# Renamed second-layer blocks, an order repaired piece by piece, and block sums on GpSimd in a channel attention and FFN kernel

## The chip, the cores and the metric

The kernel runs on one core of a Trainium2 chip. The metric is device time in microseconds, as the median of several executions; a separate profiled execution gives the trace that is read here. The engines are TensorE (PE; PEld are its weight loads), the Vector engine (DVE), the Scalar engine (ACT), GpSimd (POOL) and SyncE (SP), which issues all DMAs.

## The reference

Four batches of N = 6080 tokens with C = 256 channels go through channel attention and then a two-layer network with 2048 hidden columns, all in float32:

```python
qn = q / (np.linalg.norm(q, axis=1, keepdims=True) + 1e-06)
kn = k / (np.linalg.norm(k, axis=1, keepdims=True) + 1e-06)
s = kn.transpose(0, 2, 1) @ qn / tau
a = np.exp(s - s.max(-1, keepdims=True))
a /= a.sum(-1, keepdims=True) + 1e-09
x = (v @ a).reshape(B * N, C)
h = x @ w_in
g = 0.5 * h * (1.0 + erf(h / sqrt(2)))
return g @ w_out
```

## The kernel before

The attention matrix of a batch is folded into the first layer's weights, so that the rest is h = v (a w_in), a gelu, and g w_out. Every float32 operand is split into a high and a low half of the matmul's format, and each product is three matmuls (high by low weight, high by high, low by high weight).

Both layers use a seven-product scheme on blocks of 2 x 2 (Strassen-Winograd): each operand's blocks A11 to A22 or B11 to B22 are joined to sums S1 to S4 and T1 to T4, seven products P1 to P7 are formed in place of eight, and their sums are the result. A batch's tokens are cut into chunks of 512 or 480 tokens (twelve a batch, `CHUNKS`; the last two, from `WIDE` = 10 on, are "wide" and use plain products in the second layer), and the hidden columns into four groups g of 512 (`NWG`). One step of the main loop is one (batch b, chunk c, group g).

In a step, `chunk_ops` issues the seven first-layer products (`do`, 42 matmuls of 256 columns), whose results gather in the PSUM tiles pa or pb ("one" and "two"), px ("x") and pz ("z"). The four blocks of the gelu's input are complete in this order: x after product 3, p5 after product 4, z after product 5, "one" after product 6. Scalar applies gelu to each twice, once to the high half `his` (`gelu_hi`) and once in full to `gs` (`gelu_whole`); Vector subtracts for the low half `los` (`lo`). For the second layer there are two forms:

- *crossed*: Vector forms T1 to T4 from the four blocks in `gs` (`t_add`), Scalar casts them to high halves (`t_hi`), Vector makes the low halves (`t_lo`); the seven products take 42 matmuls of 256 columns in `chunk_out` (L1122 to L1124), with seven of the eight stored weight forms, in four loads to the ring of four `wo` tiles.
- *plain*: no T blocks; B12 gets its own high and low half, and eight products take 24 matmuls of 512 columns (L1106 to L1108), with four weight forms in two loads.

Which is used is told by `plain_out`: plain in the wide chunks, in chunk 2 of batch 0, and in the last group (g = 3) of those chunks for which `MIXED` holds, before for all. The matmuls of a step's second layer stand between the first-layer products of the next step. At a chunk's end `join_ops` sums the products' accumulators (banks po0 to po3) in the tile `osb`; where the last group is plain, two banks are read by Scalar copies and two by Vector additions, otherwise three by copies.

Beside this, v's blocks of the next chunk are summed (`v_sums`: one instruction of 512 elements and two of 256, to the tile vs, L834 to L838) and split into halves (`v_hi`, `v_lo`), the scores and norms of the next batch are formed in bursts (`burst`, `split_hi`, `split_lo`), and at a batch's end the new first-layer weights are summed (`w_adds`, four instructions of 256 elements a group, L771 to L774). All of these sums are on the Vector engine; GpSimd only writes constants at the start.

The order on each engine is made while the kernel is built. All instructions from the first weights on are recorded with their tiles (`Order.arrange`), and `schedule` runs a list planner over them: for each instruction a due time `late`, from the order of the matmuls, which is fixed; `run` plays all engines through with the planner's costs; for every stall of TensorE, `late` of the chain that caused it is set earlier, and the whole is run again, 24 times (`ROUNDS`), keeping the best order.

Of the kernel before, what the change touches and what calls it, by code (L numbers as in the profile page):

```python
# [16 lines left out]
P = 128  # L17
# [38 lines left out]
BLOCK = {(1, 0): "B22", (0, 1): "B11", (1, 1): "B21", (0, 0): "B12"}  # L56

PE, ACT, DVE, SP = (mybir.EngineType.PE, mybir.EngineType.Activation, mybir.EngineType.DVE, mybir.EngineType.SP)

# [21 lines left out]
class Order:  # L81
# [32 lines left out]
    def cost(self, ins, reads, writes):  # L114
        n = max([x[3] for x in reads + writes] + [1])
        psum = any(x[0][0] in ("pa", "pb", "px", "pz", "po0", "po1", "po2", "po3") for x in reads)
        if ins.engine == PE:
            k = reads[0][3] if reads else 1
            if ins.ins[0].dtype == F32:
                return (max(1.69 * k, 112.0),) * 2  # L120
            return max(.4167 * k + 2.8, 111.7), .4167 * k + 170
        if ins.engine == DVE:
            t = n / .96 + 66
            if len([x for x in reads if x[3] > 1]) < 2 and not psum:
                t = n / 1.92 + 66
            return t, t + 90
        if ins.engine == ACT:
            t = .855 * n + (48 if psum else 80)
            return t + 90 * (len(ins.outs) > 1), t + 105
        return 60, n * 512 / BANDWIDTH  # L130


    def arrange(self, body, start):


        todo = [i for i in body[start:] if i.engine in (PE, ACT, DVE, SP)]
        state = {}
# [47 lines left out]
    def schedule(self, todo, preds, costs):  # L185


        n = len(todo)
        self.engine = [(PE, ACT, DVE, SP).index(i.engine) for i in todo]
        self.preds, self.costs = preds, costs  # L190
# [27 lines left out]
        late = self.latest(t + 1e4)  # L218
        best = None
        for _ in range(ROUNDS):  # L220
            end, order, starts, last = self.run(late)
            if best is None or end < best[0]:
                best = end, order
            for p, q in zip(line, line[1:]):
                stall = starts[q] - starts[p] - costs[p][0]
                if stall > 30:
                    a, hops = last[q], 0
                    while a >= 0 and self.engine[a] and hops < 12:
                        late[a] -= min(1500, stall)
                        a, hops = last[a], hops + 1  # L230
        return best[1]

# [16 lines left out]

    def run(self, late):  # L250
        import heapq
        n = len(self.preds)
        left = [len(p) for p in self.preds]
        ready, starts, last = [0.0] * n, [0.0] * n, [-1] * n
        known = [[] for _ in range(4)]
        for a in range(n):
            if not left[a]:
                known[self.engine[a]].append(a)
        table = "Gelu"
        free, order, slip, dma, events = [0.0] * 4, [], 0.0, 0.0, [0.0]  # L260
        while len(order) < n:
# [3 lines left out]
            for e in range(4):  # L265
                if free[e] > now or not known[e]:
# [37 lines left out]
        return max(starts), order, starts, last  # L304


ROUNDS = 24

WAIT = {PE: 58, ACT: 34, DVE: 40, SP: 0}

# [3 lines left out]
def MIXED(b, c):  # L314
    return True

# [21 lines left out]
def channel_attention_gelu_ffn(ctx, tc, qk, kqt, vt, tau, w_in, w_out, out):  # L338
# [490 lines left out]
    def v_sums(b, c, pieces=(0, 1)):  # L829
        x, h = v_half(b, c)  # L830
        tt = nc.vector.tensor_tensor
        if 0 in pieces:
            t = vts[b, c] = pv.tile([P, 4, H], F32, name="vs")
            tt(out=t[:, 0:2, :h], in0=x[:, :, 1], in1=x[:, 0], op=ALU.subtract)  # L834
        if 1 in pieces:
            t = vts[b, c]
            tt(out=t[:, 2, :h], in0=x[:, 1, 1], in1=t[:, 0, :h], op=ALU.subtract)
            tt(out=t[:, 3, :h], in0=x[:, 1, 0], in1=t[:, 2, :h], op=ALU.subtract)  # L838
# [85 lines left out]
    def slots(n, c, g):  # L924
        at = p_slot(n, c, g)
        return {"B12": at, "B11": at + 1, "B22": 4 if c >= WIDE and g % 2 == 0 else 5, "B21": 6}

# [91 lines left out]

    SOURCE = {"B22": "x", "B11": "p5", "B21": "z", "B12": "one"}  # L1020

# [33 lines left out]
    def chunk_out(b, c, g, n):  # L1055
# [7 lines left out]
        if c >= WIDE:  # L1063
# [66 lines left out]
    def join_ops(b, c):  # L1130
# [24 lines left out]
        def join(i):  # L1155
# [4 lines left out]
            elif i == "u23":  # L1160
                tt(out=o[:, 2:4], in0=o[:, 6:4:-1], in1=p6.unsqueeze(1).broadcast_to([P, 2, h]), op=ALU.add)
            elif i == "c1":
                tt(out=o[:, 0:2], in0=banks(0), in1=o[:, 2:5:2], op=ALU.add)
            elif i == "c1s":
                tt(out=o[:, 0:2], in0=o[:, 0:2], in1=o[:, 2:5:2], op=ALU.add)
            elif i == "c22":
                tt(out=o[:, 2], in0=o[:, 2], in1=p7, op=ALU.add)
            elif i == "c2":
                tt(out=o[:, 2:4], in0=banks(1), in1=o[:, 2:4], op=ALU.add)
            elif i == "c21":  # L1170
                tt(out=o[:, 3], in0=banks(1)[:, 1], in1=o[:, 3], op=ALU.add)
            else:
# [42 lines left out]
    def narrow_unit():  # L1215
# [8 lines left out]
        else:  # L1224
# [4 lines left out]
            v = f32(wo).rearrange("p h i (c n) -> p i c h n", c=NCT)  # L1229
            for at, i, c in ((1, 0, 0), (2, 1, 0), (6, 0, 1), (7, 1, 1)):  # L1230
                keep(keep_out[form][:, at, :, q], v[:, i, c])
# [215 lines left out]
    for n, (b, c, g) in enumerate(steps):  # L1447
# [55 lines left out]
    for n, (b, c, g) in enumerate(steps):  # L1503
# [47 lines left out]
        at(e[4] + 1.85, lo, "B11")
        spread(n, "dve3", e[4] + 2.45)
        at(e[5] + .4, gelu_hi, "B21")
        at(e[5] + .9, gelu_whole, "B21")
        at(e[5] + 1.5, lo, "B21")
        at(e[6] + .1, gelu_whole, "B12")
# [73 lines left out]
```

## Time and profile before

| | before |
|---|---|
| median of 3 runs | 2036.39 us (2034.59 to 2036.76) |
| profiled execution | 2035.65 us, span of its instructions 2033.8 us |
| granted TensorE clock | 1.0 |
| DMA | 439.54 MB, mean 216 GB/s |

A profile's row names a line of the kernel, the engine, the operation, and out<-in by the program's tiles. Durations of one instruction overlap with the next on the same engine: what an instruction costs its engine is the time from its start to the next one's start in a stretch without idle time.

### The profile page before, as it was taken

How to read it: one execution, taken by the hardware profiler on the slowest of the kernel's cores; microseconds unless marked ns; L12 is line 12 of the kernel's file. 1: busy time of each engine (PE TensorE's matmuls, PEld its weight loads, DVE VectorE, ACT ScalarE, POOL GpSimd, SP SyncE). 2: the span in 40 equal slices, each digit the busy share in tenths (PEclk: the TensorE clock that was granted, in tenths of full speed). 3: DMA queues.
4: the chain of work that ended last, by engine and by line, in shares of the span. 5: the costliest groups of instructions: out<-in, count | busy, mean ns of one | idle time of the engine just before them, and what ended most of it. 6: DMA issues, size and time to landing. Idle time of an engine off the chain costs nothing.

```text
span 2033.8 us, 38744 instructions
## 1 busy us (share of the span) xinstructions
PE 2019.6 (99%) x15150; PEld 1943.7 (96%) x15150; DVE 1725.3 (85%) x2546; ACT 1577.9 (78%) x2678; POOL 0.8 (0%) x7
## 2 busy tenths in 40 slices
PE   9999999999999999999999999999999999999999
PEld 8889999999999999999999999999989999999998
DVE  6999989898598899889759999999866988988873
ACT  6668888889788888888868777777777777777764
POOL 0000000000000000000000000000000000000000
PEclk9999999999999999999999999999999999999999
DMA  9657886876476787777527666665532665665641
GB/s 375 234 169 277 282 299 233 286 246 235 151 253 233 244 272 242 270 256 261 193 100 240 200 220 213 233 221 192 196 130 83 206 220 185 198 220 184 202 149 41
DMA packets 142264, 439.54 MB, mean 216 GB/s; under 512 B 14720, under 2 KB 24960, under 8 KB 141568
## 3 DMA queue, kind: packets, MB, share of 16 engines
q1 hardware_dynamic: 142080, 437.05, 63.3%
q8 instruction: 119, 1.95, 0.4%
q14 instruction: 65, 0.53, 0.1%
HBM read 399.51 MB, written 37.49 MB: 215 GB/s over the span
## 4 chain that ended last, share of the span: by engine, by line
PE 91%; DVE 4%; DMA 3%; ACT 1%; issue 1%; SPq 0%; DVEq 0%; ACTq 0%
PE po L1122 8%; PE po L1124 8%; PE po L1123 8%; PE pb L965 4%; PE pa L965 4%; PE pa L967 4%; PE pa L966 4%; PE pb L967 4%; PE pb L966 4%; PE po L1106 3%; PE po L1108 3%; PE po L1107 3%; PE po L1081 3%; PE po L1079 3%; PE po L1080 2%; PE pa L483 2%
## 5 line engine op out<-in xcount | busy, mean ns | idle before, releaser
L998 DVE TENSOR_TENSOR los<-gs,his 128x512 fp32r<-128x512 f32 (+1 forms) x625 | 423.3, 682 | 133.7 <-ACT gs L992 107.7
L1122 PE MATMUL po<-his,wo 128*128 128x256 f32 x1554 | 427.8, 275 | 0.2 <-DMA wo<-keep_out 0.2
L1124 PE MATMUL po<-los,wo 128*128 128x256 f32 x1554 | 427.5, 275 | 0.4 <-DVE los L1016 0.4
L1123 PE MATMUL po<-his,wo 128*128 128x256 f32 x1554 | 427.4, 275 | 0.0
L1012 ACT CAST his<-gs 128x1024 fp32r<-128x1024 f32 x222 | 233.7, 1054 | 99.3 <-DVE gs L1009 98.5
L1124 PEld LDWEIGHTS po<-los,wo 128*128 128x128 f32 x1554 | 298.4, 192 | 0.6 <-DVE los L1016 0.6
L1122 PEld LDWEIGHTS po<-his,wo 128*128 128x128 f32 x1554 | 298.4, 192 | 0.4 <-issue 0.4
L1123 PEld LDWEIGHTS po<-his,wo 128*128 128x128 f32 x1554 | 298.4, 192 | 0.1
L1016 DVE TENSOR_TENSOR los<-gs,his 128x1024 fp32r<-128x1024 f32 x222 | 271.3, 1222 | 16.6 <-ACT his L1012 16.1
L965 PE MATMUL pb<-vhi,wl 128*128 128x256 f32 x760 | 209.3, 275 | 1.5 <-ACT gs L992 1.1
L965 PE MATMUL pa<-vhi,wl 128*128 128x256 f32 x760 | 208.8, 275 | 1.2 <-ACT gs L992 1.2
L966 PE MATMUL pa<-vhi,wh 128*128 128x256 f32 x760 | 209.0, 275 | 0.0
L967 PE MATMUL pa<-vlo,wh 128*128 128x256 f32 x760 | 209.0, 275 | 0.0
L966 PE MATMUL pb<-vhi,wh 128*128 128x256 f32 x760 | 209.0, 275 | 0.0
L967 PE MATMUL pb<-vlo,wh 128*128 128x256 f32 x760 | 209.0, 275 | 0.0
L995 ACT ACTIVATE his<-px 128x512 fp32r<-128x512 f32 (+1 forms) x184 | 108.7, 591 | 64.4 <-PE px L967 35.6
L1005 DVE TENSOR_TENSOR gs<-gs 128x1024 f32<-128x1024 f32 x111 | 136.0, 1225 | 26.4 <-ACT gs L992 23.5
L992 ACT ACTIVATE gs<-px 128x512 f32<-128x512 f32 (+1 forms) x184 | 109.1, 593 | 54.8 <-DVE los L1016 54.7
L965 PEld LDWEIGHTS pa<-vhi,wl 128*128 128x128 f32 x760 | 145.5, 191 | 4.6 <-ACT gs L992 1.4
L965 PEld LDWEIGHTS pb<-vhi,wl 128*128 128x128 f32 x760 | 145.6, 192 | 4.1 <-ACT gs L992 1.3
L966 PEld LDWEIGHTS pa<-vhi,wh 128*128 128x128 f32 x760 | 145.5, 192 | 3.2
L966 PEld LDWEIGHTS pb<-vhi,wh 128*128 128x128 f32 x760 | 145.6, 192 | 2.2
(315 smaller groups left out, 5500.4 us busy)
## 6 DMA issues: line engine op xcount, KB each, us to landing
wo<-keep_out SPq DMA_DIRECT2D x447, 512.0 KB, 4.6
raw<-qk SPq DMA_DIRECT2D x95, 512.0 KB, 6.6
kqc<-kqt SPq DMA_DIRECT2D x72, 512.0 KB, 5.1
wo<-keep_out SPq DMA_DIRECT2D x111, 256.0 KB, 4.1
v_raw<-vt SPq DMA_DIRECT2D x40, 512.0 KB, 5.9
out<-osb SPq DMA_DIRECT2D x40, 512.0 KB, 5.1
win<-keep_in SPq DMA_DIRECT2D x24, 512.0 KB, 4.8
raw<-w_out SPq DMA_DIRECT2D x8, 512.0 KB, 3.5
```

Source lines behind the costliest of these rows:

```text
L965: nc.tensor.matmul(o, wls[g][:, a, q], paired(vh[:, at, :h]), start=start, stop=False, skip_group_check=True)
L966: nc.tensor.matmul(o, whs[g][:, a, q], paired(vh[:, at, :h]), start=False, stop=False, skip_group_check=True)
L967: nc.tensor.matmul(o, whs[g][:, a, q], paired(vl[:, at, :h]), start=False, stop=stop, skip_group_check=True)
L992: nc.scalar.activation(out=whole(name), in_=t[SOURCE[name]], func=AF.Gelu)
L995: nc.scalar.activation(out=slot(name)[0], in_=t[SOURCE[name]], func=AF.Gelu)
L998: tt(out=slot(name)[1], in0=whole(name), in1=f32(slot(name)[0]), op=ALU.subtract)
L1005: tt(out=g4[:, 0:2], in0=g4[:, 1:3], in1=g4[:, 0:2], op=ALU.subtract)
L1012: nc.scalar.copy(out=views[1][:, 2 - 2 * i:4 - 2 * i], in_=views[0][:, 2 * i:2 * i + 2])
L1016: tt(out=views[2][:, at], in0=views[0][:, 2 * i:2 * i + 2], in1=f32(views[1][:, at]), op=ALU.subtract)
L1122: nc.tensor.matmul(o, w[:, 1, q], mh, start=starts and q == 0, stop=False, skip_group_check=True)
L1123: nc.tensor.matmul(o, w[:, 0, q], mh, start=False, stop=False, skip_group_check=True)
L1124: nc.tensor.matmul(o, w[:, 0, q], ml, start=False, stop=stops and q == 1, skip_group_check=True)
```

## The change

Blocks of the second layer get other names: what came from "x" was B22 and is B11, p5 was B11 and is B22, z was B21 and is B12, "one" was B12 and is B21. The products' order, their places in the banks and the weight forms follow. B12, which in the crossed form needs no halves of its own, is now complete after product 5, and B21 comes last. P1 now leads the crossed products, ahead of P3, and P2 stays third.

```diff
-CROSS = (("P3", "S4", "B22"), ("P1", "A11", "B11"), ("P2", "A12", "B21"), ("P7", "S3", "T3"), ("P5", "S1", "T1"),
+CROSS = (("P1", "A11", "B11"), ("P3", "S4", "B22"), ("P2", "A12", "B21"), ("P7", "S3", "T3"), ("P5", "S1", "T1"),
          ("P6", "S2", "T2"), ("P4", "A22", "T4"))
-PLACE = {"P3": (0, 0), "P2": (0, 1), "P4": (1, 1), "P1": (2, 0), "P7": (2, 1), "P5": (3, 0), "P6": (3, 1)}
+PLACE = {"P2": (0, 0), "P3": (0, 1), "P4": (1, 0), "P1": (2, 0), "P7": (2, 1), "P5": (3, 0), "P6": (3, 1)}
...
-    SOURCE = {"B22": "x", "B11": "p5", "B21": "z", "B12": "one"}
+    SOURCE = {"B11": "x", "B22": "p5", "B12": "z", "B21": "one"}
```

The plain last group stays in chunks 4 and 9 of each batch only, and two kinds of sums go to GpSimd, which the planner gets as a fifth engine:

```diff
 def MIXED(b, c):
-    return True
+    return c in (4, 9)
...
     def w_adds(tmp):
-        tt = nc.vector.tensor_tensor
+        tt = nc.gpsimd.tensor_tensor
...
     def v_sums(b, c, pieces=(0, 1)):
         x, h = v_half(b, c)
-        tt = nc.vector.tensor_tensor
+        tt = nc.gpsimd.tensor_tensor
```

The planner no longer runs the whole program 24 times. It goes forward in pieces of 160 matmuls, looks 260 further ahead, repairs the due times up to 12 times for what it sees, and then fixes the piece:

```diff
-        for _ in range(ROUNDS):
-            end, order, starts, last = self.run(late)
-            if best is None or end < best[0]:
-                best = end, order
+        while at < len(line):
+            to = min(at + STEP, len(line))
+            see = min(to + SIGHT, len(line))
+            best, trial, seen = None, list(late), line[max(0, at - 1):see]
+            for k in range(ROUNDS):
+                end = self.run(trial, state, see)
+                score = end["starts"][line[see - 1]]
+                if best is None or score < best[0] - 1:
+                    best = score, list(trial)
+                if not self.repair(trial, end, seen):
+                    break
+            late = best[1]
+            state = self.run(late, state, to)
+            at = to
...
-ROUNDS = 24
+ROUNDS, STEP, SIGHT = 12, 160, 260
```

In the crossed end of a chunk the copies of banks are placed later in the recorded order:

```diff
-            put(n + 1, "o2", copy, 0)
             put(n + 1, "o3", copy, 2)
-            put(n + 2, "act", copy, 3)
+            put(n + 1, "o5", copy, 3)
+            put(n + 1, "o5", copy, 0)
```

What that does to the engines' orders shows where a chunk of batch 3 ends. TensorE before, at the start of the last group's output (po is a bank of the output, pa and pb hold the next chunk's first products):

```order
L966 MATMUL pa<-vhi,wh_84 128x256
L967 MATMUL pa<-vlo,wh_84 128x256
L1106 MATMUL po_19170<-his,wo 128x512
L1107 MATMUL po_19170<-his,wo 128x512
L1108 MATMUL po_19170<-los,wo 128x512
L1106 MATMUL po_19170<-his,wo 128x512
L1107 MATMUL po_19170<-his,wo 128x512
L1108 MATMUL po_19170<-los,wo 128x512
```

And in the changed kernel (L994 to L996 are L965 to L967, L1151 to L1153 are L1122 to L1124 of before):

```order
L995 MATMUL pa<-vhi,wh_84 128x256
L996 MATMUL pa<-vlo,wh_84 128x256
L1151 MATMUL po_19805<-his,wo 128x256
L1152 MATMUL po_19805<-his,wo 128x256
L1153 MATMUL po_19805<-los,wo 128x256
L1151 MATMUL po_19805<-his,wo 128x256
L1152 MATMUL po_19805<-his,wo 128x256
L1153 MATMUL po_19805<-los,wo 128x256
```

The wide matmuls of the plain form are replaced by those of the crossed form.

The Vector engine in the same last group before (L998 is `lo`, L855 `v_lo`, L1159 and L1161 the join, L979 `z_add` and L982 `p5_add` of the next step, L834 a sum of `v_sums`):

```order
L998 TENSOR_TENSOR los<-gs,his 128x512 x2
L855 TENSOR_TENSOR vlo<-vs,vhi 128x512
L998 TENSOR_TENSOR los<-gs,his 128x512 x2
L1159 TENSOR_TENSOR osb<-osb 128x256
L1161 TENSOR_TENSOR osb<-osb 128x512
L979 TENSOR_TENSOR pz<-pa,p_19564 128x512
L855 TENSOR_TENSOR vlo<-vs,vhi 128x512
L855 TENSOR_TENSOR vlo<-v_raw,vhi 128x512
L834 TENSOR_TENSOR vs<-v_raw 128x512
L982 TENSOR_TENSOR p_19564<-pa,p_19564 128x512
```

And in the changed kernel (L1027 is `lo`, L884 `v_lo`, L1034, L1036 and L1038 `t_add`, L1045 `t_lo`, L1008 `z_add`, L1011 `p5_add`):

```order
L1027 TENSOR_TENSOR los<-gs,his 128x512
L884 TENSOR_TENSOR vlo<-vs,vhi 128x512
L1027 TENSOR_TENSOR los<-gs,his 128x512
L1034 TENSOR_TENSOR gs<-gs 128x1024
L1027 TENSOR_TENSOR los<-gs,his 128x512
L1036 TENSOR_TENSOR gs<-gs 128x512
L1045 TENSOR_TENSOR los<-gs,his 128x1024
L1038 TENSOR_TENSOR gs<-gs 128x512
L1008 TENSOR_TENSOR pz<-pa,p_20204 128x512
L884 TENSOR_TENSOR vlo<-vs,vhi 128x512
L1045 TENSOR_TENSOR los<-gs,his 128x1024
L1011 TENSOR_TENSOR p_20204<-pa,p_20204 128x512
```

The last group now has the T blocks' additions and splits; the sum on vs has left the queue, the join comes a step later, and the first `t_add` stands ahead of the last `lo`. GpSimd, which had nothing there, has three rows a chunk:

```order
L863 TENSOR_TENSOR vs<-v_raw 128x512
L866 TENSOR_TENSOR vs<-v_raw,vs 128x256
L867 TENSOR_TENSOR vs<-v_raw,vs 128x256
```

More of the change, by code (lines that the diff above doesn't have):

```diff
@@ L50 @@
 FORMS = ("S4", "A11", "A12", "S3", "S1", "S2", "A21", "A22")
-CROSS = (("P3", "S4", "B22"), ("P1", "A11", "B11"), ("P2", "A12", "B21"), ("P7", "S3", "T3"), ("P5", "S1", "T1"),
+CROSS = (("P1", "A11", "B11"), ("P3", "S4", "B22"), ("P2", "A12", "B21"), ("P7", "S3", "T3"), ("P5", "S1", "T1"),
          ("P6", "S2", "T2"), ("P4", "A22", "T4"))
 SLOT = {"T2": 0, "T4": 1, "T1": 2, "T3": 3, "B11": 4, "B22": 5, "B21": 6}
-PLACE = {"P3": (0, 0), "P2": (0, 1), "P4": (1, 1), "P1": (2, 0), "P7": (2, 1), "P5": (3, 0), "P6": (3, 1)}
+PLACE = {"P2": (0, 0), "P3": (0, 1), "P4": (1, 0), "P1": (2, 0), "P7": (2, 1), "P5": (3, 0), "P6": (3, 1)}
 GSLOT = {"B11": 0, "B12": 1, "B22": 2, "B21": 3}
-BLOCK = {(1, 0): "B22", (0, 1): "B11", (1, 1): "B21", (0, 0): "B12"}
-PE, ACT, DVE, SP = (mybir.EngineType.PE, mybir.EngineType.Activation, mybir.EngineType.DVE, mybir.EngineType.SP)
+BLOCK = {(1, 0): "B11", (0, 1): "B22", (1, 1): "B12", (0, 0): "B21"}
+PE, ACT, DVE, SP, POOL = (mybir.EngineType.PE, mybir.EngineType.Activation, mybir.EngineType.DVE, mybir.EngineType.SP,
+                          mybir.EngineType.Pool)
 RINGS = {"raw": 3, "hl": 2, "wo": 4, "win": 2, "rden": 2}
@@ L129, in cost @@
             return t + 90 * (len(ins.outs) > 1), t + 105
+        if ins.engine == POOL:
+            return 3.65 * n + 60, 3.65 * n + 150
         return 60, n * 512 / BANDWIDTH
     def arrange(self, body, start):
-        todo = [i for i in body[start:] if i.engine in (PE, ACT, DVE, SP)]
+        todo = [i for i in body[start:] if i.engine in (PE, ACT, DVE, SP, POOL)]
         state = {}
@@ L188, in schedule @@
         n = len(todo)
-        self.engine = [(PE, ACT, DVE, SP).index(i.engine) for i in todo]
+        self.engine = [(PE, ACT, DVE, SP, POOL).index(i.engine) for i in todo]
         self.preds, self.costs = preds, costs
@@ L218, in schedule, with repair, begin @@
         late = self.latest(t + 1e4)
-        best = None
-        for _ in range(ROUNDS):
-            end, order, starts, last = self.run(late)
-            if best is None or end < best[0]:
-                best = end, order
[L224 to L231, printed above, removed]
+        state, at = self.begin(), 0
+        while at < len(line):
[12 more added lines that the diff above has]
+            at = to
+        return self.run(late, state, n + 1)["order"]
+    def repair(self, late, end, line):
+        found = False
+        starts, last = end["starts"], end["last"]
+        for p, q in zip(line, line[1:]):
+            stall = starts[q] - starts[p] - self.costs[p][0]
+            if stall > 30:
+                a, hops, found = last[q], 0, True
+                while a >= 0 and self.engine[a] and hops < 12:
+                    late[a] -= min(1500, stall)
+                    a, hops = last[a], hops + 1
+        return found
+    def begin(self):
+        n = len(self.preds)
+        left = [len(p) for p in self.preds]
+        known = [[] for _ in range(5)]
+        for a in range(n):
+            if not left[a]:
+                known[self.engine[a]].append(a)
+        return {"left": left, "ready": [0.0] * n, "starts": [0.0] * n, "last": [-1] * n, "known": known,
+                "free": [0.0] * 5, "order": [], "slip": 0.0, "dma": 0.0, "events": [0.0], "table": "Gelu", "passes": 0}
     def latest(self, end):
@@ L248, in latest, with run @@
         return late
-    def run(self, late):
+    def run(self, late, state, until):
         import heapq
         n = len(self.preds)
[L253 to L261, printed above, removed]
+        left, ready, starts, last, free, order, events = (
+            list(state[x]) for x in ("left", "ready", "starts", "last", "free", "order", "events"))
+        known = [list(x) for x in state["known"]]
+        slip, dma, table, passes = (state[x] for x in ("slip", "dma", "table", "passes"))
+        while len(order) < n and passes < until:
             now = heapq.heappop(events)
@@ L264, in run @@
                 heapq.heappop(events)
-            for e in range(4):
+            for e in range(5):
                 if free[e] > now or not known[e]:
@@ L293, in run @@
                     slip = now - self.nominal[pick]
+                    passes += 1
                 if e == 3:
@@ L303, in run @@
                         heapq.heappush(events, max(now, ready[b]))
-        return max(starts), order, starts, last
-ROUNDS = 24
-WAIT = {PE: 58, ACT: 34, DVE: 40, SP: 0}
+            if passes >= until:
+                heapq.heappush(events, now)
+        return {"left": left, "ready": ready, "starts": starts, "last": last, "known": known, "free": free, "order": order,
+                "slip": slip, "dma": dma, "events": events, "table": table, "passes": passes}
+ROUNDS, STEP, SIGHT = 12, 160, 260
+WAIT = {PE: 58, ACT: 34, DVE: 40, SP: 0, POOL: 60}
 BANDWIDTH, DMA_LAT, DMA_LATE, TABLE, BACKLOG = 320.0, 3000, 7000, 1290, 2200
 def MIXED(b, c):
-    return True
+    return c in (4, 9)
 NARROWS = (4, 9)
@@ L925, in slots @@
         at = p_slot(n, c, g)
-        return {"B12": at, "B11": at + 1, "B22": 4 if c >= WIDE and g % 2 == 0 else 5, "B21": 6}
+        return {"B21": at, "B22": at + 1, "B11": 6 if c >= WIDE and g % 2 == 0 else 4, "B12": 5}
     def chunk_ops(b, c, g, n):
@@ L1160, in join @@
             elif i == "u23":
[L1161 removed]
+                tt(out=o[:, 2:4], in0=o[:, 5:7], in1=p6.unsqueeze(1).broadcast_to([P, 2, h]), op=ALU.add)
             elif i == "c1":
[L1163 removed]
+                tt(out=o[:, 0:2], in0=banks(0), in1=o[:, 4:2:-1], op=ALU.add)
             elif i == "c1s":
[L1165 removed]
+                tt(out=o[:, 0:2], in0=o[:, 0:2], in1=o[:, 4:2:-1], op=ALU.add)
             elif i == "c22":
[L1167 removed]
+                tt(out=o[:, 3], in0=o[:, 3], in1=p7, op=ALU.add)
             elif i == "c2":
@@ L1170, in join @@
             elif i == "c21":
-                tt(out=o[:, 3], in0=banks(1)[:, 1], in1=o[:, 3], op=ALU.add)
+                tt(out=o[:, 2], in0=banks(1)[:, 0], in1=o[:, 2], op=ALU.add)
             else:
@@ L1229, in narrow_unit @@
             v = f32(wo).rearrange("p h i (c n) -> p i c h n", c=NCT)
-            for at, i, c in ((1, 0, 0), (2, 1, 0), (6, 0, 1), (7, 1, 1)):
+            for at, i, c in ((1, 1, 0), (2, 0, 0), (6, 1, 1), (7, 0, 1)):
                 keep(keep_out[form][:, at, :, q], v[:, i, c])
@@ L1546, in channel_attention_gelu_ffn @@
         spread(n, "o5", ends[5] + .05)
-        spread(n, "o2", ends[2] + .05)
         spread(n, "o3", ends[3] + .05)
-        at(e[4] + .8, gelu_hi, "B11")
-        at(e[4] + 1.3, gelu_whole, "B11")
-        at(e[4] + 1.85, lo, "B11")
+        at(e[4] + .8, gelu_hi, "B22")
+        at(e[4] + 1.3, gelu_whole, "B22")
+        at(e[4] + 1.85, lo, "B22")
         spread(n, "dve3", e[4] + 2.45)
[L1553 to L1556, printed above, removed]
+        at(e[5] + .1, gelu_whole, "B12")
         if plain_out(b, c, g):
-            at(e[6] + .6, gelu_hi, "B12")
-            at(e[6] + 1.2, lo, "B12")
+            at(e[5] + .4, gelu_hi, "B12")
+            at(e[5] + 1.5, lo, "B12")
+        at(e[6] + .1, gelu_hi, "B21")
+        at(e[6] + .6, gelu_whole, "B21")
+        if plain_out(b, c, g):
+            at(e[6] + 1.2, lo, "B21")
         else:
             at(e[6] + .7, t_add, 0)
+            at(e[6] + 1.2, lo, "B21")
             at(e[6] + 1.85, t_hi, 0)
@@ L1585, in channel_attention_gelu_ffn @@
     todo, preds, costs = order.arrange(list(body), opened)
-    latest = {e: [i.name for i in list(body)[:opened] if i.engine == e] for e in (PE, ACT, DVE, SP)}
+    latest = {e: [i.name for i in list(body)[:opened] if i.engine == e] for e in (PE, ACT, DVE, SP, POOL)}
     for at in order.schedule(todo, preds, costs):
```

12 lines of the change are left out of this document (6 added, 6 removed).

## The prediction

> **What bounds the kernel now.** I read the page's head and its chain first, then the waits of TensorE, then windows over single stages, then instruction starts on the Vector engine.
>
> ```profile
> span 2033.8 us, 38744 instructions
> ...
> PE 2019.6 (99%) x15150; PEld 1943.7 (96%) x15150; DVE 1725.3 (85%) x2546; ACT 1577.9 (78%) x2678; POOL 0.8 (0%) x7
> ...
> PE 91%; DVE 4%; DMA 3%; ACT 1%; issue 1%; SPq 0%; DVEq 0%; ACTq 0%
> ```
>
> TensorE (PE) carries 91% of the chain that ended last; GpSimd (POOL) does nothing after the start. The waits of TensorE say how much of its time is not work (columns: who waited for whom, total us, times, longest):
>
> ```profile
> PE pa L965 <- ACT gs L992: 1.2, 1, 1.2
> PE pb L965 <- ACT gs L992: 1.1, 1, 1.1
> ...
> PE po L1081 <- DVE los L998: 0.6, 1, 0.6
> PE po L1124 <- DVE los L1016: 0.4, 1, 0.4
> PE pb L965 <- DVE pz L979: 0.3, 1, 0.3
> ```
>
> Together 3.6 us in the steady part. So a matmul saved there is time saved, as long as the Vector engine (DVE), second at 85%, keeps up. How close it is needs stages. These windows (length, then busy time and instructions by engine; clock, DMA share, GB/s) are one plain output group, three crossed ones, the whole chunk that they make in the last batch, and a long stage of batch 2 which also prepares the next batch:
>
> ```profile
> 1723.81:1733.68 9.87, 9.87 (x69) 9.23 (x67) 7.62 (x13) 7.44 (x14) 0.00 (x0) 1.00 0.60 211
> 1733.68:1761.82 28.14, 28.14 (x255) 28.14 (x253) 26.21 (x37) 21.19 (x35) 0.00 (x0) 1.00 0.66 217
> 1723.81:1761.82 38.01, 38.01 (x321) 37.37 (x319) 33.82 (x49) 28.63 (x49) 0.00 (x0) 1.00 0.65 215
> 1048.00:1490.00 442.00, 442.00 (x3614) 433.13 (x3614) 397.65 (x557) 338.19 (x559) 0.00 (x0) 1.00 0.62 209
> ```
>
> TensorE is busy throughout, at full clock; the Vector engine 33.82 of 38.01 us and 90% of the long stage.
>
> **Plain to crossed in the last group: the gain.** MIXED was true for every chunk under 10 and is now true for chunks 4 and 9. Chunks 3, 5, 6, 7, 8 of batch 0 and eight chunks in each of three batches change: 5 + 24 = 29. The plain group takes 9.87 us of TensorE, a crossed one 28.14 / 3 = 9.38 (84 matmuls of 256 columns, 0.1117 us each). 29 x 0.49 = 14.2 us less, all of it on the path. The same from counts:
>
> ```profile
> L1122 PE MATMUL po<-his,wo 128*128 128x256 f32 x1554 | 427.8, 275 | 0.2 <-DMA wo<-keep_out 0.2
> ...
> L1106 PE MATMUL po<-his,wo 128*128 128x512 f32 x328 | 125.4, 382 | 0.0
> ```
>
> In the change's order the first stands 1960 times and the second 96. With the two sister lines, 1218 matmuls of 256 columns come and 696 of 512 go. Their durations (275 and 382 ns) overlap, so I price by windows: six layer-two products of 42 matmuls against 24 wide ones, as above.
>
> **What the Vector engine gets and loses.** Its durations overlap too, so I count from start to start (start, duration):
>
> ```profile
> 1735.54 1.23 DVE L1016 TENSOR_TENSOR los<-gs,his 128x1024 fp32r<-128x1024 f32 x1
> 1736.68 0.69 DVE L1009 TENSOR_TENSOR gs<-gs 128x512 f32<-128x512 f32 x1
> 1737.29 0.69 DVE L979 TENSOR_TENSOR pz<-pb,p 128x512 f32<-128x512 f32 x1
> 1737.89 0.68 DVE L1169 TENSOR_TENSOR osb<-po,osb 128x512 f32<-128x512 f32 x1
> ...
> 1747.36 0.68 DVE L834 TENSOR_TENSOR vs<-v_raw 128x512 f32<-128x512 f32 x1
> ...
> 1756.71 0.42 DVE L855 TENSOR_TENSOR vlo<-v_raw,vhi 128x256 fp32r<-128x256 f32 x1
> 1757.05 0.42 DVE L838 TENSOR_TENSOR vs<-v_raw,vs 128x256 f32<-128x256 f32 x1
> 1757.38 1.22 DVE L1016 TENSOR_TENSOR los<-gs,his 128x1024 fp32r<-128x1024 f32 x1
> ...
> 1761.07 0.68 DVE L855 TENSOR_TENSOR vlo<-vs,vhi 128x512 fp32r<-128x512 f32 x1
> ```
>
> 1024 elements occupy it 1.14 us, 512 0.60, 256 0.34. A crossed group is seven of 512 (z, p5, three lo, two t_add) and three of 1024 (a t_add, two t_lo): 4.20 + 3.42 = 7.62 us. A plain one is six of 512: 3.60. A chunk's vlo rows are 3 x 0.60 + 0.34 = 2.14, v's sums 0.60 + 2 x 0.34 = 1.28, the join 3 x 0.60 + 2 x 0.34 = 2.48 (plain end) or 2 x 0.60 + 3 x 0.34 = 2.22 (crossed end).
>
> - Before: 3 x 7.62 + 3.60 + 2.14 + 1.28 + 2.48 = 32.4 of 38.0 us, 5.6 spare.
> - After: 4 x 7.62 + 2.14 + 2.22 = 34.8 of 4 x 9.38 = 37.5 us, 2.7 spare.
>
> Where the next batch's scores are prepared, each three groups add two rows of 1024 and one of 512 (2.88 us) on the Vector engine and 24 matmuls (2.68 us) on TensorE:
>
> ```profile
> L473 DVE TENSOR_TENSOR hl<-raw,hl 128x1024 fp32r<-128x1024 f32 x66 | 79.9, 1218 | 0.6 <-ACT hl L469 0.5
> L493 DVE TENSOR_TENSOR sacc<-pb,sacc 128x512 f32<-128x512 f32 x16 | 11.0, 686 | 0.4
> ```
>
> By chunk that is 3.84 and 3.57 us, so 38.7 of 41.1: 2.4 spare. The work still fits, at 93 to 94%, where before it stood at 85 to 87%. The waits that it had, 3.6 us in all, I let grow as the spare time shrinks, by about 5.6 / 2.7: to 7.2 us, so 3.6 us more. That is the second term. Waits could also fall, since the order is now repaired in pieces; the low bound has them all gone.
>
> **The sums on GpSimd.** 38 chunks times three sums and 16 groups times four. No row shows an addition on this engine. Its nearest rows:
>
> ```profile
> masks.py:199 POOL TENSOR_SCALAR_AFFINE_SELECT ident<-ident 128x128 f32<-128x128 f32 x1 | 0.3, 292 | 0.1
> L374 POOL MEMSET ones<- 128x128 f32 x1 | 0.2, 204 | 0.3 <-POOLq L1621 0.3
> ```
>
> The select reads one operand, 292 ns for 128 elements; scaled, a chunk's 1024 elements take 2.3 us. That is my lower end; with two operands read one after the other, 4.7 us is the upper one. I take 3.5, between them, since reading is likely a part of the select's cost and not all. The Trainium skill (GPSIMD Engine Reference, Performance versus the Vector engine) gives 4497 ns for 2048 elements, by which a chunk would take an estimated 2.2 us. As latency the sums cost nothing: in the rows above the first sum starts at 1747.36 and its low half is split at 1761.07, 13.7 us later, against the 2 to 3.5 us by which the chain grows. The cover is that gap; without it the next chunk's first products would come late by the difference. The weights' sums (16 x 4 x 256 elements, 0.58 to 1.2 us each) sit where the wide chunks leave the Vector engine far idler. What GpSimd may take from the Vector engine by running beside it is the doubt; no row of before can show it. It lies between nothing and the sums' whole length; the main case is that it stays under the spare 2.4 us a chunk, where it costs nothing, and beyond that it is the first rival.
>
> **Small parts.** The Scalar engine (ACT) gets 58 casts and 29 copies and loses 29 gelus:
>
> ```profile
> L1012 ACT CAST his<-gs 128x1024 fp32r<-128x1024 f32 x222 | 233.7, 1054 | 99.3 <-DVE gs L1009 98.5
> ...
> L995 ACT ACTIVATE his<-pz 128x512 fp32r<-128x512 f32 x152 | 89.8, 591 | 7.2 <-PE pz L967 4.9
> ...
> L1148 ACT COPY osb<-po 128x512 f32<-128x512 f32 x75 | 43.3, 580 | 0.3 <-DVE win L624 0.3
> ```
>
> 2 x 1.05 + 0.58 - 0.59 = 2.1 us a chunk on top of 28.63 in 37.5: hidden, at 82%. SyncE issues two more loads for each group, 29 of 512 KB and 29 of 256 KB, 23 MB on 440, into a ring of four:
>
> ```profile
> wo<-keep_out SPq DMA_DIRECT2D x447, 512.0 KB, 4.6
> ...
> wo<-keep_out SPq DMA_DIRECT2D x111, 256.0 KB, 4.1
> ```
>
> Four loads a crossed group have had to land every 9.38 us already, 28 us on end, and TensorE waited 0.2 us for them in all (the L1122 row): 0, or at worst one landing, 4 us, where the order lets a load wait.
>
> The new names let the block that needs no own high half (B12) come from the product before the last, so the block differences start 12 matmuls, 1.3 us, earlier; B21, now last, has five items of 0.67 us until the third output product asks for it, and needs two gelus and one lo, about 1.8 us. Nothing on the path: 0, with 1.5 us as cover.
>
> **Sum.** -14.2 + 3.6 = -10.6 us. The profiled execution took 2035.65 us (span 2033.8 and 1.85 around it), 0.7 below the median 2036.39; against the median that makes 2025.8.
>
> **Rivals.** *GpSimd holds the Vector engine.* If Vector instructions with both operands in SBUF wait while a GpSimd one reads, 85% of the chunk's 34.8 us is exposed (z, p5 and one join read PSUM). At 3.5 us a chunk it loses 3.0, against 2.4 to 2.7: 0.3 to 0.6 over, and blocks of over 1 us arrive at once while t_lo is awaited, so I price 0.55 a chunk, 29 x 0.55 = 16: 2042. At 4.7 us it loses 4.0, 29 x 1.5 = 44: 2070. The gain is gone when the holding exceeds the spare time by 0.37 us (10.6 / 29), at about 3.4 us of GpSimd a chunk. Against it stands only that the length is unknown. The Trainium skill (SBUF — State Buffer, Who interferes with whom) says that such a pair does contend, and that the one which starts first holds the shared port for its whole instruction; no run shown here has the two side by side.
>
> *The spare time isn't usable.* In three crossed groups the Vector engine is idle 28.14 - 26.21 = 1.93 us, mostly behind gelus, 0.64 a group. Four such groups are 2.6 us, the whole of the spare 2.4 to 2.7. If these waits can't be filled, each chunk falls behind by some 0.4 us: 29 x 0.4 = 12 us, about the gain: 2036 to 2038. For it speaks that the queue is in order; against it that before had 90% over 442 us without a stall.
>
> *The change only moves work.* If the crossed group were already limited by something else there would be no gain; the two windows, both with TensorE full, exclude it, and I give it 0.02.
>
> **Chances.** Main case 0.58, all of it faster by over 0.2% (4 us, about what can be told from no change). GpSimd holding 0.24, slower. Spare time not usable 0.16: within 0.2% 0.13, faster 0.02, slower 0.01. No gain 0.02, within. So 0.60, 0.15, 0.25. Range: the low end is 2036.4 - 14.2 - 3.6 = 2018.6 (all waits gone), taken as 2018; above, it reaches over the second rival and the first at its middle price, to 2046. Left out is the first rival from there on, about 0.12, and 0.04 below.
>
> **What would show it.** Crossed windows of 9.38 us four in a row with TensorE full; L1122's sister at x1960; Vector rows still 683 ns for 512 while GpSimd runs. Lengthened Vector rows, or waits of layer-two matmuls for los over 20 us, would show me wrong, and GpSimd rows over 1.7 us for 512 elements would say by what.

## The result

The changed kernel took 2064.17 us (median of 4 runs, 2061.49 to 2065.47) against 2036.58 for the kernel before beside it: a ratio of 1.0137, 95% interval 1.0124 to 1.0149. It is 28 us slower, where 11 us faster was forecast, and lies above the range. Head and chain of the profile after:

```profile
span 2059.7 us, 40243 instructions
...
PE 2021.6 (98%) x15672; PEld 1951.2 (95%) x15672; DVE 1807.3 (88%) x2484; ACT 1612.2 (78%) x2734; POOL 215.6 (10%) x185
...
PE 77%; DVE 12%; ACT 4%; issue 4%; DMA 2%; POOL 0%; SPq 0%; DVEq 0%; ACTq 0%
```

TensorE's share of the chain fell from 91 to 77%, the Vector engine's rose from 4 to 12. GpSimd itself has 0% of it. TensorE's idle time in all rose from 14.2 us (span less busy time, 2033.8 - 2019.6) to 38.1, and its busy time rose by 2.0 us where 14.2 less were forecast. Its longest waits, which were 3.6 us together in the steady part before:

```profile
PE pb L994 <- DVE pz L1008: 9.2, 14, 1.0
PE po L1153 <- DVE los L1045: 4.5, 6, 1.6
PE pa L994 <- DVE pz L1008: 4.2, 8, 1.0
```

L994 is the next first-layer product into a PSUM tile that `z_add` (L1008) still reads. The windows of the last batch show where the gain is and where it goes (three crossed groups; one crossed group; two; one):

```profile
1661.91:1690.05 28.14, 28.14 (x255) 28.14 (x254) 26.75 (x37) 23.52 (x40) 2.00 (x2) 1.00 0.77 255
1690.05:1701.22 11.17, 10.18 (x87) 9.61 (x86) 10.87 (x14) 6.75 (x12) 2.49 (x2) 1.00 0.52 161
1701.22:1719.98 18.76, 18.76 (x171) 18.76 (x170) 18.12 (x24) 16.27 (x29) 4.33 (x3) 1.00 0.71 226
1719.98:1730.13 10.15, 9.68 (x87) 9.49 (x86) 9.94 (x15) 7.23 (x13) 0.00 (x0) 1.00 0.57 194
```

Five groups take the forecast 9.38 us. The second and fourth window take 11.17 and 10.15. The second begins within one set of GpSimd's sums (1687.97 to 1692.62), the fourth just behind the next (which ends at 1719.8), and the Vector engine is busy nearly throughout in both. What these sums did to the Vector engine stands in its groups and GpSimd's:

```profile
L863 POOL TENSOR_TENSOR vs<-v_raw 128x512 f32<-128x512 f32 x38 | 63.4, 1668 | 1355.3 <-DMA v_raw<-vt 475.2 <-DVE vlo L884 466.7 <-DVE small L727 95.9
L867 POOL TENSOR_TENSOR vs<-v_raw,vs 128x256 f32<-128x256 f32 x38 | 45.0, 1185 | 3.0
L866 POOL TENSOR_TENSOR vs<-v_raw,vs 128x256 f32<-128x256 f32 x38 | 42.7, 1122 | 3.0
```

```profile
L1045 DVE TENSOR_TENSOR los<-gs,his 128x1024 fp32r<-128x1024 f32 x280 | 349.7, 1249 | 35.1 <-ACT his L1041 33.5
L1027 DVE TENSOR_TENSOR los<-gs,his 128x512 fp32r<-128x512 f32 x468 | 340.6, 734 | 25.8 <-ACT gs L1021 21.2 <-ACT his L1024 2.7
...
L1038 DVE TENSOR_TENSOR gs<-gs 128x512 f32<-128x512 f32 x140 | 102.1, 729 | 0.1
...
L1008 DVE TENSOR_TENSOR pz<-pa,p 128x512 f32<-128x512 f32 x76 | 52.5, 691 | 1.9 <-PE pa L996 1.9
...
L1011 DVE TENSOR_TENSOR p<-pa,p 128x512 f32<-128x512 f32 x76 | 52.0, 684 | 4.2 <-PE pa L996 4.2
```

The same Vector groups in the kernel before (L998 is L1027, L1016 is L1045, L1009 is L1038, L979 is L1008):

```profile
L998 DVE TENSOR_TENSOR los<-gs,his 128x512 fp32r<-128x512 f32 x497 | 340.1, 688 | 71.2 <-ACT gs L992 60.0 <-ACT his L995 3.3
L1016 DVE TENSOR_TENSOR los<-gs,his 128x1024 fp32r<-128x1024 f32 x222 | 271.3, 1222 | 16.6 <-ACT his L1012 16.1
...
L1009 DVE TENSOR_TENSOR gs<-gs 128x512 f32<-128x512 f32 x111 | 76.0, 684 | 0.3
L979 DVE TENSOR_TENSOR pz<-pa,p 128x512 f32<-128x512 f32 x76 | 52.7, 693 | 5.6 <-PE pa L967 5.4
```

Rows with both operands in SBUF got longer (L1027 from 688 to 734 ns on average, L1045 from 1222 to 1249, L1038 from 684 to 729); rows that read PSUM did not (L1008 693 before, 691 now).

### The profile page after: what moved, and what is told of

Read it like the earlier page. It is cut to its first block, busy times and chain, and to the rows that moved or that the text cites. A ratio compares the mean times of both kernels' runs of the same rounds, so it can differ in the third digit from the quotient of the medians.

```text
span 2059.7 us, 40243 instructions
## 1 busy us (share of the span) xinstructions
PE 2021.6 (98%) x15672; PEld 1951.2 (95%) x15672; DVE 1807.3 (88%) x2484; ACT 1612.2 (78%) x2734; POOL 215.6 (10%) x185
## 4 chain that ended last, share of the span: by engine, by line
PE 77%; DVE 12%; ACT 4%; issue 4%; DMA 2%; POOL 0%; SPq 0%; DVEq 0%; ACTq 0%
PE po L1153 9%; PE po L1151 9%; PE po L1152 9%; PE pb L994 4%; PE pa L994 4%; PE pb L996 3%; PE pb L995 3%; PE pa L996 3%; PE pa L995 3%; PE po L1110 2%; PE po L1108 2%; PE po L1109 2%; PE pa L512 2%; PE pb L512 2%; PE pz L996 1%
## 5 line engine op out<-in xcount | busy, mean ns | idle before, releaser
L1153 PE MATMUL po<-los,wo 128*128 128x256 f32 x1960 | 541.3, 276 | 5.7 <-DVE los L1045 4.5
L1151 PE MATMUL po<-his,wo 128*128 128x256 f32 x1960 | 540.2, 276 | 0.5 <-DVE osb L1200 0.4
L1152 PE MATMUL po<-his,wo 128*128 128x256 f32 x1960 | 539.2, 275 | 0.0
L1027 DVE TENSOR_TENSOR los<-gs,his 128x512 fp32r<-128x512 f32 (+1 forms) x596 | 428.2, 725 | 97.7 <-ACT gs L1021 62.8
L1041 ACT CAST his<-gs 128x1024 fp32r<-128x1024 f32 x280 | 294.7, 1053 | 143.3 <-DVE gs L1038 122.0
L1153 PEld LDWEIGHTS po<-los,wo 128*128 128x128 f32 x1960 | 376.2, 192 | 9.0 <-DVE los L1045 7.9
L1045 DVE TENSOR_TENSOR los<-gs,his 128x1024 fp32r<-128x1024 f32 x280 | 349.7, 1249 | 35.1 <-ACT his L1041 33.5
L1151 PEld LDWEIGHTS po<-his,wo 128*128 128x128 f32 x1960 | 376.2, 192 | 1.1 <-DVE osb L1200 1.0
L1152 PEld LDWEIGHTS po<-his,wo 128*128 128x128 f32 x1960 | 376.3, 192 | 0.1
L994 PE MATMUL pb<-vhi,wl 128*128 128x256 f32 x760 | 211.2, 278 | 10.5 <-DVE pz L1008 9.2
L994 PE MATMUL pa<-vhi,wl 128*128 128x256 f32 x760 | 210.7, 277 | 6.5 <-DVE pz L1008 4.2
L996 PE MATMUL pa<-vlo,wh 128*128 128x256 f32 x760 | 209.1, 275 | 0.0
L996 PE MATMUL pb<-vlo,wh 128*128 128x256 f32 x760 | 209.0, 275 | 0.0
L863 POOL TENSOR_TENSOR vs<-v_raw 128x512 f32<-128x512 f32 x38 | 63.4, 1668 | 1355.3 <-DMA v_raw<-vt 475.2
L1034 DVE TENSOR_TENSOR gs<-gs 128x1024 f32<-128x1024 f32 x140 | 173.8, 1241 | 5.6 <-ACT gs L1021 5.3
L1024 ACT ACTIVATE his<-p 128x512 fp32r<-128x512 f32 (+1 forms) x184 | 115.8, 629 | 65.1 <-DVE p L1011 64.6
L994 PEld LDWEIGHTS pb<-vhi,wl 128*128 128x128 f32 x760 | 145.7, 192 | 14.7 <-DVE pz L1008 12.3
L994 PEld LDWEIGHTS pa<-vhi,wl 128*128 128x128 f32 x760 | 145.7, 192 | 10.5 <-DVE pz L1008 6.2
```

The source lines that it names most:

```text
L994: nc.tensor.matmul(o, wls[g][:, a, q], paired(vh[:, at, :h]), start=start, stop=False, skip_group_check=True)
L996: nc.tensor.matmul(o, whs[g][:, a, q], paired(vl[:, at, :h]), start=False, stop=stop, skip_group_check=True)
L1024: nc.scalar.activation(out=slot(name)[0], in_=t[SOURCE[name]], func=AF.Gelu)
L1027: tt(out=slot(name)[1], in0=whole(name), in1=f32(slot(name)[0]), op=ALU.subtract)
L1034: tt(out=g4[:, 0:2], in0=g4[:, 1:3], in1=g4[:, 0:2], op=ALU.subtract)
L1041: nc.scalar.copy(out=views[1][:, 2 - 2 * i:4 - 2 * i], in_=views[0][:, 2 * i:2 * i + 2])
```

## The experiments

Theory H: a GpSimd instruction that reads SBUF holds the Vector engine, and that stalls TensorE. Rivals: C, the Vector engine is too full for crossed groups on end in any case; T, it is the later arrival of the sums; R, names or planner. Times are medians; ratios are to the kernel before, run on the same chip. The planner makes the engines' order anew for each kernel, so a part of a difference can be the order's, except where the text says that the order was the same.

### Parts of the change undone

Both sums back on the Vector engine; then the same with plain last groups everywhere, with GpSimd and without:

```diff
-        tt = nc.gpsimd.tensor_tensor
+        tt = nc.vector.tensor_tensor
```
```diff
-    return c in (4, 9)
+    return True
```

Sums on the Vector engine, crossed groups:

> The changed kernel with both kinds of sums back on the Vector engine; names, planner and crossed groups stay. Theory H (a GpSimd sum holds the Vector engine, and its lumps stall TensorE): the stalls that came go away, 2036.5 - 14.2 = 2022 plus at most 5, so 2020 to 2028, Vector rows of 512 back at 684 ns. Theory C (the Vector engine is too full for crossed groups on end, with or without GpSimd): it now has 1.3 us a chunk more, 36.1 of 37.5 us, so no faster than the change, 2060 or more.

Measured 2041.91 us, ratio 1.0031 (1.0018 to 1.0044): between the two. Without GpSimd 22 us of the change's time go, but the kernel is still slower than before.

Sums on GpSimd, plain groups:

> The changed kernel with the plain last group in every chunk again; the sums stay on GpSimd. H: the same 71 us of lengthened Vector rows as in the change, but into 5.6 + 1.3 us of spare time a chunk, so part of the stalls stays: 2040 to 2055, slower than before. C: the Vector engine is relieved, 2030 to 2037.

Measured 2058.55 us, ratio 1.0114 (1.0097 to 1.0131). H, with a little more than its band: GpSimd costs 23.6 us even where the Vector engine had 5.6 us a chunk to spare and was relieved of 1.3.

Sums on the Vector engine, plain groups:

> New names and the planner in pieces alone: plain last groups everywhere, all sums on the Vector engine. H and C: as before, 2032 to 2038. A third theory R (the new names or the new planner's order cost the time): 2050 or more.

Measured 2034.96 us, ratio 0.9994 (0.9984 to 1.0003). So of the three parts, GpSimd's sums cost 22 to 24 us with either kind of group, the crossed groups 7 in place of gaining 14, and names and planner nothing where the groups stay plain.

One stretch of a trace shows how. These are the Vector engine, then GpSimd, TensorE and the Scalar engine (start, duration) in the kernel with plain groups and sums on GpSimd:

```profile
1754.92 1.51 DVE L1196 TENSOR_TENSOR osb<-osb 128x256 f32<-128x256 f32 x1
1756.36 1.75 DVE L1045 TENSOR_TENSOR los<-gs,his 128x1024 fp32r<-128x1024 f32 x1
1758.03 1.21 DVE L1038 TENSOR_TENSOR gs<-gs 128x512 f32<-128x512 f32 x1
1759.16 0.69 DVE L1008 TENSOR_TENSOR pz<-pb,p 128x512 f32<-128x512 f32 x1
```

```profile
1754.50 1.65 POOL L863 TENSOR_TENSOR vs<-v_raw 128x512 f32<-128x512 f32 x1 [40.10 <-DVE los L1027]
1756.23 0.80 POOL L866 TENSOR_TENSOR vs<-v_raw,vs 128x256 f32<-128x256 f32 x1
1757.10 1.59 POOL L867 TENSOR_TENSOR vs<-v_raw,vs 128x256 f32<-128x256 f32 x1
```

```profile
1759.90 0.38 PE L994 MATMUL pb<-vhi,wl 128*128 128x256 f32 x1 [1.03 <-DVE pz L1008]
```

```profile
1759.27 1.05 ACT L1041 CAST his<-gs 128x1024 fp32r<-128x1024 f32 x1 [3.29 <-DVE gs L1038]
```

Three Vector rows in a row are longer than they are alone: 1.51 for 0.42 us, 1.75 for 1.22, 1.21 for 0.68, together 2.15 us. `z_add`, which is not lengthened itself (0.69), starts that much later, and TensorE waits 1.03 us for it; the Scalar engine waits 3.29, a part of which it would have waited anyway. It is not the only place: TensorE is without a matmul for 23.1 us in this kernel, and 12.7 of them lie between the start of a set of sums of v's blocks and 6 us behind its end, which is a fifth of the time. The kernel with plain groups and all sums on the Vector engine has 9.0 us in all.

### Which of the two sums

> The changed kernel with only the sums of v's blocks on GpSimd, the weights' sums back on the Vector engine. H: the three sums a chunk are 4.0 of the 5.7 us that GpSimd is busy per chunk on average, and lie in the crossed chunks, so two thirds or more of the 42 us of stalls stay: 2048 to 2060. C: 2062 or more.

Measured 2063.67 us, ratio 1.0141 (1.0126 to 1.0156): above H's band and, as a number, in C's (2062 or more); but C alone had been ruled out by the 2041.91 without GpSimd. It is the same as the change, so the weights' sums cost nothing. The reverse, only the weights' sums on GpSimd:

> The kernel at 2041.9 with only the weights' sums on GpSimd. They hold the Vector engine too (15 of the 71 us lengthened), but where plain wide chunks leave it idle: 2040 to 2045. If every hold stalls TensorE: 2047 to 2052.

Measured 2041.69 us, ratio 1.0034 (1.0025 to 1.0044), the 2041.9 of the kernel without GpSimd: the Vector rows beside them grew by 14 us in all, and that cost no time.

### Reading, writing, or being late

In the kernel at 2041.9, GpSimd first writes vs, or first computes it, and the Vector engine then writes it again:

```diff
             t = vts[b, c] = pv.tile([P, 4, H], F32, name="vs")
+            nc.gpsimd.memset(t[:, 0:2, :h], 0.0)
+            nc.gpsimd.memset(t[:, 2, :h], 0.0)
+            nc.gpsimd.memset(t[:, 3, :h], 0.0)
             tt(out=t[:, 0:2, :h], in0=x[:, :, 1], in1=x[:, 0], op=ALU.subtract)
```

> The kernel with the sums on the Vector engine (2041.9) in which GpSimd first writes constants over the same parts of vs, three writes a chunk of the same sizes, at the same point. H (reading by GpSimd holds the Vector engine): no hold, 2040 to 2045. Theory T (it is the later start of vs, through one more engine, that costs): about as much as the change, 2055 to 2066.

Measured 2042.35 us, ratio 1.0038 (1.0025 to 1.0051), in H's band. The 2662 rows of the Vector engine come in the same order as in the kernel at 2041.9, so the writes are the only difference. For the second, the three writes are the sums with `nc.gpsimd.tensor_tensor`:

> The same, but GpSimd computes the sums of v's blocks into vs, and then the Vector engine computes them again over them. Beside the previous kernel only the reading by GpSimd is added; the Vector engine's own work is that of the kernel at 2041.9. H: 22 us or more above that, 2062 to 2075. T: the same as the kernel with writes, within 4 us.

Measured 2085.52 us, ratio 1.0248 (1.0233 to 1.0263): 43 us more than with writes, beyond H's band. The planner gives a write and a sum on GpSimd the same cost, and 96% of the Vector engine's rows keep their order between the two kernels. Two rows of each, writes first:

```profile
L863 POOL MEMSET vs<- 128x512 f32 x38 | 20.1, 529 | 1844.5 <-DVE vlo L887 1477.9 <-DVE vlo L913 175.5 <-DVE rden L728 88.7
```

```profile
L1030 DVE TENSOR_TENSOR los<-gs,his 128x512 fp32r<-128x512 f32 x468 | 317.5, 685 | 22.9 <-ACT gs L1024 19.4 <-ACT his L1027 0.9
```

```profile
L864 POOL TENSOR_TENSOR vs<-v_raw 128x512 f32<-128x512 f32 x38 | 72.1, 1896 | 1769.0 <-DVE vlo L888 743.1 <-DMA v_raw<-vt 573.7 <-DVE los L1031 94.6
```

```profile
L1031 DVE TENSOR_TENSOR los<-gs,his 128x512 fp32r<-128x512 f32 x468 | 332.4, 716 | 20.5 <-ACT gs L1025 16.9 <-ACT his L1028 1.0
```

With writes the Vector rows keep their 685 ns, with sums they grow to 716. T falls for a wait on one more engine as such, since writes brought that too; but the sums take over three times as long as the writes, so a part of these 43 us may be their lateness. The waits of TensorE say that it is a small one. With sums it waits this long for the low halves of v's blocks, 0.6 us of which came with writes too:

```profile
PE px L1000 <- DVE vlo L888: 1.3, 2, 0.7
PE pa L1000 <- DVE vlo L888: 0.6, 1, 0.6
```

In the change itself TensorE's matmuls wait for none of them. Why the reading costs 43 us here and 22 in the change is not shown; here the Vector engine still does all its own sums.

### Shorter holds

In the kernel at 2058.6, each sum of v's blocks is cut into pieces of 128 elements:

```diff
-            tt(out=t[:, 0:2, :h], in0=x[:, :, 1], in1=x[:, 0], op=ALU.subtract)
+            for k in range(2):
+                for a in range(0, h, h // 2):
+                    w = slice(a, a + h // 2)
+                    tt(out=t[:, k, w], in0=x[:, k, 1, w], in1=x[:, 0, k, w], op=ALU.subtract)
```

> The kernel with plain last groups and the sums on GpSimd (2058.6), with the sums of v's blocks cut into eight pieces of 128 elements in place of one of 512 and two of 256. If it is the length of a single hold that stalls TensorE: the stalls fall to half or less, 2036 to 2047. If it is the held time in all, or the number of holds: 2054 or more.

Measured 2049.25 us, ratio 1.0068 (1.0054 to 1.0081), between the bands: of 23.6 us, 14.3 are left. But the cut also shortened the holds in all: taking each Vector row that overlaps a sum of v's blocks against the median of its like alone, they are 51 us with whole sums and 34 with pieces, a third less, where the cost fell by 39%. So this run does not tell the length of one hold from the held time.

### How full the Vector engine may be

The sums of v's blocks left out:

```diff
-            t = vts[b, c] = pv.tile([P, 4, H], F32, name="vs")
-            tt(out=t[:, 0:2, :h], in0=x[:, :, 1], in1=x[:, 0], op=ALU.subtract)
...
+            vts[b, c] = state["vs"]
```

> Leaves the sums of v's blocks out (vs holds a constant), all else as in the kernel at 2041.9: the Vector engine then has the 34.8 us a chunk of the prediction, with nothing held. If the prediction's step on spare time was right: 2022 to 2028. Theory C' (a queue in order already stalls TensorE at 93%): 2030 to 2040.

Measured 2020.14 us, ratio 0.9928 (0.9912 to 0.9945). The gain of the crossed groups is all there: 15.0 us below the kernel before beside it. Batch 2 in this kernel, and in the one at 2041.9:

```profile
1071.00:1500.00 429.00, 428.56 (x3695) 424.42 (x3694) 401.26 (x556) 342.61 (x566) 0.00 (x0) 1.00 0.69 229
```

```profile
1071.00:1515.00 444.00, 439.93 (x3750) 433.59 (x3749) 421.16 (x595) 351.35 (x578) 0.00 (x0) 1.00 0.67 223
```

The Vector engine is busy 93.5% here, 94.9% there; TensorE idles 0.4 us here, 4.1 there. So 1.3 us of Vector work a chunk, 49 us in all, is worth 22 us of time, though the sum of work still fits (36.1 of 37.5 us). C is right as well, at 96% by start-to-start sums and not at 93%. How much of the 22 us is the load is not shown, since this run changes two more things: the splits of v's blocks no longer wait for their sums, and the planner put the Vector engine's rows in another order.

### Fewer crossed groups, sums on the Vector engine

```diff
-    return c in (4, 9)
+    return c % 2 == 0 or c == 9
```

> Sums on the Vector engine, the last group crossed in every second chunk only (15 groups in place of 29): gain 15 x 0.49 = 7.4 us against 2035.0. If the stalls of crossed groups on end need several chunks to build up, nearly all of it comes: 2028 to 2031. If each crossed chunk stalls by itself: 2036 to 2039.

Measured 2028.97 us, ratio 0.9968 (0.9955 to 0.9981): in the first band, and faster than both kernels: a crossed chunk between plain ones hardly stalls. Two crossed chunks of three:

> Sums on the Vector engine, plain last group in chunks 1, 4, 7 and 9: 22 crossed in place of 15 (2029.0) or 29 (2041.9). If a chunk's plain end lets the Vector engine make up for the two before it: 2035.0 - 22 x 0.49 = 2024 plus 2, so 2024 to 2028. If the second crossed chunk in a row already stalls: 2030 to 2037.

Measured 2030.52 us, ratio 0.9977 (0.9967 to 0.9987), at the lower edge of the second band: seven more crossed groups bring nothing more. And more of them in the last batch only:

> Sums on the Vector engine; every second chunk crossed as at 2029.0, but in the last batch, which prepares no scores for a next one, all but chunks 4 and 9: 19 crossed groups. By the stalls seen there at 2041.9 (about 2 us for eight chunks): 2029.0 - 4 x 0.49 + 1 to 2 = 2028 to 2030.

Measured 2029.38 us, ratio 0.9970 (0.9959 to 0.9980). The three can't be told apart.

### Names or planner

The kernel before with MIXED alone changed:

> The kernel before with one edit, the plain last group in chunks 4 and 9 alone; old names, old planner, sums on the Vector engine. If the crossing by itself costs what it did with the new planner (2041.9): 2039 to 2046. If the new names and planner helped: 2048 or more. If they hurt: 2036 or less.

Measured 2069.32 us, ratio 1.0167 (1.0154 to 1.0181): with the old names and planner the crossed groups cost 34 us, in the second band. The new names with the old repair over the whole program:

```diff
+        for _ in range(24):
+            end = self.run(late, self.begin(), n + 1)
+            score = max(end["starts"])
+            if best is None or score < best[0]:
+                best = score, end["order"]
+            self.repair(late, end, line)
+        return best[1]
```

> Sums on the Vector engine, new names and crossed groups as at 2041.9, but the due times repaired over the whole program 24 times, as before the change. If the names made the difference to 2069.3: 2039 to 2047. If the repair in pieces did: 2060 to 2070.

Measured 2043.91 us, ratio 1.0044 (1.0029 to 1.0059), in the band of the names. TensorE's waits for the second layer's low halves, old names first (L1124 is L1145, L998 is L1019, L1016 is L1037):

```profile
PE po L1124 <- DVE los L998: 8.4, 7, 1.8
PE po L1124 <- DVE los L1016: 6.5, 13, 1.8
```

```profile
PE po L1145 <- DVE los L1037: 4.5, 7, 1.0
...
PE po L1145 <- DVE los L1019: 1.9, 1, 1.9
```

The names, with the recorded order and the places of the copies that go with them, are worth 25 us once groups are crossed; the repair in pieces (2041.9) can't be told from the old one.

## Why the prediction was wrong, step by step

**The gain on TensorE** was right: 9.38 us for a crossed group, 14.2 us in all, 15.0 measured where nothing disturbs it.

**The Vector engine's spare time, without GpSimd** was right in the case summed. At 34.8 us a chunk no stall was added (2020.1; the 3.6 us put in for them were not needed, and 3.6 x 5.6 / 2.7 makes 7.5 and not 7.2, which changes the forecast by 0.3 us). The step has a narrow edge that I did not see: at 36.1 us, with 1.4 still free, 22 us are lost, though not by the load alone as far as the run shows. The second rival named this mechanism, and it happened in the kernel with the sums on the Vector engine.

**The length of the sums** was mis-sized a little: 3.5 us a chunk taken, 1668 + 1122 + 1185 = 3975 ns measured, inside the bounds of 2.3 and 4.7. The 2.2 us estimated beside it from the Trainium skill are too low: even the shortest rows in the change's trace, 1.27 us for 512 elements and twice 0.73 for 256, make 2.7.

**The step that failed** is the treatment of the holding: that it "stays under the spare 2.4 us a chunk, where it costs nothing". Its amount did stay under. The rows of L1027, L1045 and L1038 grew by 468 x 46 + 280 x 27 + 140 x 45 ns = 35 us, about 0.9 us for each of the 38 sets of sums; all rows beside these sums, each against the median of its like alone, grew by 56 us, 1.5 us a set and at most 2.2. Yet the kernel lost 22 to 24 us with 2.4 us a chunk free and with 5.6. The holds come in one lump, 2.15 us in the rows at 1754.92, in a queue that runs in order, ahead of a `z_add`. TensorE waits 1.03 us for that one, so the queue had about 1.1 us of slack there. The prediction counted `z_add` as exempt, since it reads PSUM, and looked for waits for los; but it stands behind the held rows, and TensorE's waits for it are the longest in the change: 9.2 + 4.2 us, with 4.5 for the los of L1045. Spare time a chunk is a mean; what a lump meets is the slack of the next instruction that is waited for. The first rival put its price and its turning point (3.4 us of GpSimd a chunk) on the same mean, so it had the holding right and the way to the stall wrong. That the measured 2064 lies in its 2042 to 2070 is luck: by its reckoning plain groups, with 5.6 us a chunk to spare, would lose nothing, and they lost 23.6. Its chance of 0.24 was too low.

The rule cited there (the Trainium skill, SBUF — State Buffer, Who interferes with whom) agrees with this case's rows. Vector rows with two SBUF operands wait (0.68 becomes 1.21 us) where GpSimd was there first, `z_add` and `p5_add` with one in PSUM do not (691 and 684 ns), and GpSimd instructions that only write don't disturb (685 ns beside 529 ns writes).

**The names** were booked at nothing. For plain groups that is measured (2035.0 against 2036.1). Under crossed groups they carry 25 us (2069.3 to 2043.9), and TensorE's waits for the second layer's low halves fall from 14.9 to 6.4 us. That the 1.5 us booked as cover made this difference is likely, but not shown.

**Scalar engine and loads** stayed hidden: ACT at 78%, no wait for the loads of wo among TensorE's longest.

## What to carry to other kernels

Moving work from a full engine to one whose reads hold it need not relieve it: here each chunk took 1.3 us off the Vector queue, put 1.5 us of holding on it (2.2 at most), and some of that stood in front of the instruction on which TensorE waits. Compare a hold with the slack of the next awaited instruction and not with the engine's mean spare time. Near 95% of an in-order engine a part of the change may bring what the whole does not: fifteen crossed groups in place of 29 gave 2029.0 us.

## What was not expected of the hardware

The division is sharp. GpSimd reading SBUF lengthened a Vector row of 256 elements from 0.42 to 1.51 us; GpSimd writing the same tile lengthened none. In the change's trace, 131 of the 134 Vector rows with both operands in SBUF that began while a GpSimd sum had over 0.1 us to run are longer than their like alone; of the 30 with an operand in PSUM none is.

GpSimd waits too, and longer. In the kernel where both engines compute the sums (Vector rows, then GpSimd's):

```profile
754.48 0.68 DVE L1031 TENSOR_TENSOR los<-gs,his 128x512 fp32r<-128x512 f32 x1
755.08 0.68 DVE L888 TENSOR_TENSOR vlo<-v_raw,vhi 128x512 fp32r<-128x512 f32 x1
755.68 0.68 DVE L1040 TENSOR_TENSOR gs<-gs 128x512 f32<-128x512 f32 x1
756.28 0.41 DVE L1200 TENSOR_TENSOR osb<-osb 128x256 f32<-128x256 f32 x1
756.62 1.21 DVE L1049 TENSOR_TENSOR los<-gs,his 128x1024 fp32r<-128x1024 f32 x1
757.75 0.69 DVE L1012 TENSOR_TENSOR pz<-pa,p 128x512 f32<-128x512 f32 x1
758.35 1.17 DVE L1042 TENSOR_TENSOR gs<-gs 128x512 f32<-128x512 f32 x1
```

```profile
754.10 4.87 POOL L864 TENSOR_TENSOR vs<-v_raw 128x512 f32<-128x512 f32 x1 [27.25 <-DVE vlo L888]
```

Five Vector rows with both operands in SBUF run on end at their usual length beside this sum, which takes 4.87 us where the shortest took 1.27. The next Vector row with two SBUF operands behind `z_add` (L1012), which reads PSUM, is held: 1.17 for 0.68 us.
